# Expert tiles of an attention and expert kernel in pairs of 64-row halves, with copied words between the halves and moved weight tiles

## The chip, the core and the metric

The kernel runs on one core of a Trainium2 chip. The metric is the time of one execution on the device in microseconds (us). TensorE (PE) multiplies matrices, VectorE (DVE), ScalarE (ACT) and GpSimd (POOL) do the rest, SyncE (SP) issues most of the DMAs. Each engine works through its own instructions in order; semaphores order the engines among each other. Products go to banks of PSUM, eight in all, of 2 KB a partition.

## What is computed

An attention without softmax over 8 batches of 2496 rows, and a layer of 8 experts over all 19968 rows, each row going to the one expert with the highest logit:

```python
scores = (1.0 / S) * np.matmul(z, z.transpose(0, 2, 1))      # z: 8 x 2496 x 64
x = u * np.matmul(np.maximum(scores, 0.0) ** 2, v)           # u, v: 8 x 2496 x 256
logits = x @ w_gate + modality_bias[modality_id]             # 19968 x 8
e_idx = np.argmax(logits, axis=1)                            # gate_w: softmax at e_idx
h = np.maximum(x[mask] @ w1[e], 0.0)                         # mask: rows of expert e
out[mask] = gate_w[mask, None] * (h @ w2[e])                 # w1: 256 x 1024, w2: 1024 x 256
```

All is fp32. The kernel keeps each operand as a high part, rounded to PE's fast fp32 format, and a low part, what is left, and makes a product as three: high by high, high by low and low by high.

## The kernel before

**Attention** takes some 1340 us. A batch is cut into 5 chunks of 512 rows (the last has 448), a chunk into 10 steps. A step makes scores (`scores`, L279, three pairs), squares them, splits them into `ah` and `al` (L287 to L318), and sums products with `v` (`weigh`, L334, twelve pairs). All of these come as pairs: two matmuls, one on partitions 0 to 63 of its operands and one on 64 to 127, each to a bank of its own, so that both work at once on the two halves of PE's rows. The sums of the two banks are added when they are evacuated (L378 by ACT, L382 by DVE). A planner, which runs while the program is written, keeps a clock for ACT and DVE and gives each step a `limit` for them; what fits is issued there, the rest waits. Among that work are the logits (L434), the routing, and the split of the first experts' weights. Rows of x go to per-expert buckets `xs` in DRAM by indirect DMAs of POOL (L547).

**The experts** take the rest: 39 whole tiles of 512 rows of one expert, numbered -4 to 34, and a remainder that `run_quarter` and `run_tile` do. The tiles -4 to -1 run while the last batch's routing goes on; `between` and `put` hang pieces of it (on DVE and POOL) behind steps of these tiles. For a tile SP fetches rows (`fetch`, `xg`, L792), the 2 MB of weights of a tile two later (`fetch_weights`, L811 and L815), DVE turns the rows (`turn_blocks`, L853), and ACT and DVE split rows (`part_high` L860, `part_low` L865) and weights (L831, L835) in the course of the tile before. There are three sets of weight tiles `w1_n`, `w2_n`.

`run_tile` goes through eight slices f of 128 hidden columns. `up(t, f)` makes six products over all 128 rows of PE to one bank (L1005): two blocks of the 256 inputs by three terms, 512 columns each. ACT rectifies the sum to `hh` (L1009), DVE takes the rest to `hl` (L1010). Two slices later `down` follows for the four blocks j of 128 rows: `hh` by both parts of w2, 512 columns (L1018), and `hl` by the high part, 256 columns (L1019), into the block's bank `po`, which sums over all eight slices. So 48 + 32 products of 512 columns and 32 of 256 columns make a tile. `finish` multiplies by the gate (ACT L1033, DVE L1035), and POOL writes the rows by indirect DMAs (L1037). The engines keep the order in which the program is written there.

The first expert tile, -4, begins when the last chunk of attention ends; that chunk's rows are turned on PE by `make_last_rows` (L394, eight transposes of all 128 rows to two banks) behind the second slice.

## Time and profile before

| what | value |
| --- | --- |
| median of three runs | 2245.33 us (2245.01 to 2245.93) |
| the profiled execution's own time | 2245.74 us |
| its span in the profile | 2243.9 us |
| PE busy | 2221.6 us, 99% |
| DVE, ACT, POOL busy | 80%, 70%, 16% |
| granted clock of PE, mean | 0.997 of full speed |
| attention, without its first 20 us | 1320 us, PE busy 1319.32 |
| steady expert tiles, 1455 to 2225 us | 770 us, PE busy 770.00 |

The profile's page gives each engine's busy time, the granted clock in 40 slices, the chain of work that ended last, and the costliest groups of instructions. A timeline lists the instructions of one engine with their start, length and the idle time before them. Matmuls overlap in the pipeline of PE: a matmul of 512 columns is listed with about 390 ns, and the next one starts some 230 ns after it. What one costs is read from start to start.

### The profile page before, as it was taken

To read this page: it belongs to the slowest core of one execution; us is meant where nothing else is said; L and a number is where in the kernel's file an instruction comes from. 1 tells how busy PE (TensorE), PEld (TensorE's weight loads), DVE (VectorE), ACT (ScalarE), POOL (GpSimd) and SP (SyncE) were. 2 spreads that over 40 slices of the span, in tenths; PEclk is the share of its full clock that TensorE was granted. 3 is DMA by queue.
4 is the path that set the end of the run, shared out by engine and by line. 5 is a ranking of instruction groups with operands and counts; after the bars stand their busy time and mean duration, and the time that the engine had idled before them with its cause. 6 is when DMAs were issued, how large, how long until landed. Compare 5 with 4: busy or idle time off the path is not lost.

```text
span 2243.9 us, 44470 instructions
## 1 busy us (share of the span) xinstructions
PE 2221.6 (99%) x16874; PEld 2020.7 (90%) x16874; DVE 1804.4 (80%) x4552; ACT 1573.0 (70%) x1917; POOL 366.3 (16%) x349
## 2 busy tenths in 40 slices
PE   9999999999999999999999999999999999999996
PEld 7889999999999999999999888888888888888885
DVE  7889989989989989989989998666666666666663
ACT  7888888888888888888888873455555555555452
POOL 0000220220210210220220422211111111111111
PEclk9999999999999999999999999999999999999998
DMA  5222223222012112112111122754545454545440
GB/s 184 111 70 101 83 89 110 79 74 79 32 59 75 35 57 76 35 56 75 39 45 40 51 88 62 187 158 126 157 128 155 127 155 130 152 134 149 135 140 23
DMA packets 199602, 216.64 MB, mean 97 GB/s; under 512 B 118448, under 2 KB 166064, under 8 KB 194512
## 3 DMA queue, kind: packets, MB, share of 16 engines
q1 hardware_dynamic: 184288, 172.49, 26.3%
q0 software_dynamic: 15088, 41.21, 5.0%
q8 instruction: 134, 2.20, 0.4%
q14 instruction: 92, 0.75, 0.1%
HBM read 168.23 MB, written 62.19 MB: 103 GB/s over the span
## 4 chain that ended last, share of the span: by engine, by line
PE 59%; issue 25%; DMA 9%; POOL 3%; DVE 3%; ACT 1%; POOLq 0%; DVEq 0%; ACTq 0%
PE acc L334 44%; PE s L279 12%; DMA out_dram<-y,ids 9%; POOL out_dram L1037 3%; DVE spare L434 1%; PE ph L1005 1%; PE po L412 1%; PE po L1018 1%; DVE al L318 1%; PE po L1019 0%; DVE vl L249 0%; POOLq L1037 0%; PE warm L886 0%; DVE ah L309 0%; DVE x L382 0%
## 5 line engine op out<-in xcount | busy, mean ns | idle before, releaser
L287 ACT ACTIVATE r<-s 128x1024 f32<-128x1024 f32 (+1 forms) x395 | 397.8, 1007 | 184.5 <-PE s L279 182.7
L318 DVE TENSOR_TENSOR al<-r,ah 128x1024 fp32r<-128x1024 f32 (+1 forms) x359 | 429.8, 1197 | 84.1 <-ACT ah L309 68.9
L334 PE MATMUL acc<-ah,vh 64*128 64x512 f32 (+1 forms) x3120 | 492.8, 383 | 1.0 <-DVE ah L301 1.0
L334 PE MATMUL acc<-ah,vl 64*128 64x512 f32 (+1 forms) x3120 | 487.0, 382 | 0.0
L334 PE MATMUL acc<-al,vh 64*128 64x512 f32 (+1 forms) x3120 | 483.8, 381 | 0.0
L434 DVE SCALAR_TENSOR_TENSOR spare<-x,wgb 128x256 f32<-128x256 f32 x1280 | 462.4, 421 | 1.0
L1009 ACT ACTIVATE hh<-ph 128x512 fp32r<-128x512 f32 x312 | 186.6, 598 | 388.2 <-PE ph L1005 348.1
L1018 PE MATMUL po<-w,hh 128*128 128x512 f32 x1256 | 450.0, 394 | 0.0
L1005 PE MATMUL ph<-xh,w 128*128 128x512 f32 x1248 | 430.1, 395 | 1.4 <-DVE x L382 1.4
L293 ACT ACTIVATE r<-r 128x1024 f32<-128x1024 f32 (+1 forms) x399 | 415.6, 1042 | 3.5
L334 PEld LDWEIGHTS acc<-ah,vh 64*128 64x128 f32 x3120 | 383.3, 184 | 17.7 <-ACT x L378 1.7
L334 PEld LDWEIGHTS acc<-al,vh 64*128 64x128 f32 x3120 | 383.0, 184 | 14.6
L334 PEld LDWEIGHTS acc<-ah,vl 64*128 64x128 f32 x3120 | 381.3, 184 | 15.0 <-DVE vl L249 0.2
L1010 DVE SCALAR_TENSOR_TENSOR hl<-ph,hh 128x512 fp32r<-128x512 f32 x312 | 215.7, 691 | 219.5 <-ACT hh L1009 191.8
L279 PE MATMUL s<-zm 64*128 64x512 f32 (+1 forms) x2400 | 388.8, 386 | 0.8 <-ACT r L287 0.3
L547 POOL DMA_INDIRECT xs<-x,sloti x160 | 206.5, 1291 | 1016.2 <-DVE x L545 971.9
L1019 PE MATMUL po<-w,hl 128*128 128x256 f32 x1256 | 351.5, 280 | 0.2 <-DVE hl L1010 0.2
L279 PEld LDWEIGHTS s<-zm 64*128 64x128 f32 x2400 | 292.6, 185 | 12.3 <-ACT r L287 0.8
L309 ACT CAST ah<-r 128x1024 fp32r<-128x1024 f32 (+1 forms) x283 | 288.1, 1018 | 0.0
L1005 PEld LDWEIGHTS ph<-xh,w 128*128 128x128 f32 x1248 | 234.2, 188 | 57.6 <-DVE x L382 1.8
L1018 PEld LDWEIGHTS po<-w,hh 128*128 128x128 f32 x1256 | 235.7, 188 | 55.4
L1037 POOL DMA_INDIRECT out_dram<-y,ids x157 | 152.8, 974 | 693.7 <-DVE y L1035 659.2
(155 smaller groups left out, 1979.4 us busy)
## 6 DMA issues: line engine op xcount, KB each, us to landing
w<-w1s SPq DMA_DIRECT2D x37, 1024.0 KB
w<-w2s SPq DMA_DIRECT2D x37, 1024.0 KB
xg<-xs SPq DMA_DIRECT2D x156, 128.0 KB
vr<-in_v_dram SPq DMA_DIRECT2D x32, 512.0 KB
ut<-in_u_dram SPq DMA_DIRECT2D x32, 512.0 KB
zr<-in_zt_dram SPq DMA_DIRECT2D x40, 256.0 KB
w1s<-in_moe_w_dram SPq DMA_DIRECT2D x16, 512.0 KB
w2s<-in_moe_w_dram SPq DMA_DIRECT2D x8, 1024.0 KB
```

The lines of the kernel that those rows point to most:

```text
L279: nc.tensor.matmul(out=s[t][:, :w], lhsT=lhs, rhs=mv[halves[t], ql, :w], start=n == 0, stop=n == 2)
L287: nc.scalar.activation(out=r[:, :, :w], in_=both[:, :, :w], func=AF.Relu, scale=INV)
L293: nc.scalar.square(out=a[:, :, :w], in_=a[:, :, :w])
L309: copy(out=ah[:, :, :w], in_=st_a[g][:, :, :w])
L318: nc.vector.tensor_tensor(out=al[:, :, :w], in0=a[:, :, :w], in1=ah[:, :, :w].bitcast(F32), op=ALU.subtract)
L334: nc.tensor.matmul(out=acc[b, c][r][dh][:, :w], lhsT=V[b, k // J][y][halves[r], k % J, dh * P:(dh + 1) * P], rhs=x[halves[r], k % 2, :w], ...
L434: nc.vector.scalar_tensor_tensor(out=spare[:, k % 2, :], in0=x[:, j, 0:D], scalar=1.0, in1=wgb[:, e, :], op0=ALU.mult, op1=ALU.mult, accum ...
L1005: nc.tensor.matmul(out=ph, lhsT=lhs, rhs=rhs[:, k, :], start=n == 0, stop=n == 3 * KD - 1)
L1010: nc.vector.scalar_tensor_tensor(out=hl, in0=ph, scalar=0.0, in1=hh.bitcast(F32), op0=ALU.max, op1=ALU.subtract)
L1018: nc.tensor.matmul(out=po[j], lhsT=hh[:, s], rhs=both, start=f == 0, stop=False, skip_group_check=True)
L1019: nc.tensor.matmul(out=po[j][:, 0:D], lhsT=hl[:, s], rhs=w[:, 0, :], start=False, stop=f == KF - 1, skip_group_check=True)
L1037: nc.gpsimd.indirect_dma_start(out=out, out_offset=bass.IndirectOffsetOnAxis(ap=ids[:, j:j + 1], axis=0), in_=y, in_offset=None, bounds_ch ...
```

## The change

Every whole tile is done by a new function, `run_whole`; `run_tile` stays for the remainder.

- **Halves.** `up_half` makes two slices g and g+1 together, in pairs: one matmul on rows 0 to 63 for one slice and one on rows 64 to 127 for the other, each to its slice's bank. After six pairs (`d` = 0) each bank has half of its sum; six more pairs (`d` = 1), with the halves swapped, give the other half. `down_half` does the same with two blocks of rows and their banks `po`, for two to four slices in a go. A tile has 80 pairs of 512 columns and 32 of 256.
- **The copied word.** `change` issues on ACT a copy of one word that waits for the last matmul of a half; the first matmul of the other half on these banks waits for the copy. There are 7 in a tile, 273 in all.
- **The order.** `UPS` and `DOWNS` set it: other slices' products stand between the two halves of a bank. The last two pieces of a tile's downs run within the next tile, behind its first two halves of ups; `finish` goes with the second. In the last tile they follow at once.
- **Weights** of tile t+2 are fetched behind the second of these pieces; the split of rows and weights is hung on other steps.
- **Addresses.** The weight tiles stood at addresses that leave 32 in a division by 64 bytes, and now stand at multiples of 64 (a small tile `room` and a fourth buffer of `ids` move them). `xh`, `xl`, `hh` and `hl` stand at multiples of 64 in both.
- **Rows of the last chunk** are turned by `make_rows` in 16 transposes of 64 rows, behind the first half of ups of tile -4.
- **Start.** The strip of zeros for the warm-up is set by POOL (128 columns) and DVE (the rest); the warm-up has four pairs of 128 columns ahead of seven of 512, where it had eight of 512; the second half of z is prepared earlier.
- **Planner.** Narrower limits for DVE at the last chunk of a batch; no logits are issued in the last step of attention, they go to the first expert tiles.

```diff
-    nc.vector.memset(zeros.bitcast(F32), 0.0)
+    few = 128
+    nc.gpsimd.memset(zeros[:, 0:few].bitcast(F32), 0.0)
+    nc.vector.memset(zeros[:, few:T].bitcast(F32), 0.0)
...
+        pool.tile([P, 8], F32, name="room")
         fetch_weights(-1)
...
-        for n in range(8):
+        for n in 4 * [few] + 7 * [T]:
...
+                if f is logits and g == G - 1:
+                    continue
...
+            if c == NCH - 1 and i == NI - 3 and b < B - 1:
+                limit["D"] = after + 2.0
             if i >= NI - 2:
-                limit.update(A=after + 0.2, D=after + (0.6 if i == NI - 1 else 2.0))
+                limit.update(A=after + 0.2, D=after + (0.6 if i == NI - 1 else 1.0 if c == NCH - 1 and b < B - 1 else 2.0))
...
+    def product(out, lhs, rhs, r, key, start, stop):
+        m = ins_of(nc.tensor.matmul(out=out, lhsT=lhs, rhs=rhs, start=start, stop=stop, skip_group_check=True))
+        if key in writer and writer[key][0] != r:
+            tc.add_manual_dep(m, writer[key][1].name, data, reason="the other half's sums")
+            del writer[key]
...
+    def change():
+
+        i = ins_of(nc.scalar.copy(out=one_of[:, 0:1], in_=one_of[:, 1:2]))
+        tc.add_manual_dep(i, ended[0].name, data, reason="products of one half")
+        for key in open_keys:
+            writer[key][1] = i
+        open_keys.clear()
+
+    def up_half(t, g, d, banks):
+
+        _, xh, xl = TL[t]
+        w = weights_of(t)[0]
+        terms = [(k, q, x) for k in range(KD) for q, x in ((0, xh), (0, xl), (1, xh))]
+        for n, (k, q, x) in enumerate(terms):
+            for r, rows_of in enumerate(halves):
+                i = (r + d) % 2
+                c = slice((g + i) * P, (g + i + 1) * P)
+                product(
+                    banks[i], w[rows_of, q, k, c], x[rows_of, k, :], r, (t, "h", g + i),
+                    n == 0 and not d, n == len(terms) - 1 and d == 1,
+                )
+
+    def down_half(t, fs, h, po, d):
+
+        for p in range(0, J, 2):
+            for f in fs:
+                hh, hl = h[f]
+                w = weights_of(t)[1][:, f]
+                for x, y in ((hh, w.rearrange("p h d -> p (h d)")), (hl, w[:, 0, :])):
+                    for r, rows_of in enumerate(halves):
+                        i = p + (r + d) % 2
+                        product(
+                            po[i][:, 0:y.shape[1]], x[rows_of, i * P:(i + 1) * P], y[rows_of], r, (t, "o", i),
+                            f == 0 and not d and x is hh, f == KF - 1 and not d and x is hl,
+                        )
...
+    UPS = [(0, 0), (0, 1), (2, 0), (4, 0), (2, 1), (4, 1), (6, 0), (6, 1)]
+    DOWNS = {3: ((0, 1), 0), 4: ((0, 1), 1), 5: ((2, 3), 1), 6: ((2, 3), 0), 7: ((4, 5), 0)}
+    behind = []
+
+    def run_whole(t, ahead, extra={}):
...
+        for f, (g, d) in enumerate(UPS):
+            if not d:
+                banks[g] = [ps_h.tile([P, T], F32, tag="h", name="ph") for _ in halves]
+            up_half(t, g, d, banks[g])
+            if d:
+                h.update({g + i: rectify(x, T) for i, x in enumerate(banks.pop(g))})
+            elif f != 2:
+                change()
+            parts = {0: (0, 1), 3: (2,), 7: (3,)}.get(f, ()) if ahead and t >= -1 else ()
...
+            if behind and f < 2:
+                behind.pop(0)()
+            if f == 1 and t >= 0 and t + 2 < min(UNC + 1, MAXT):
+                fetch_weights(t + 2)
+            if f in DOWNS:
...
+                fs, d = DOWNS[f]
+                down_half(t, fs, h, po, d)
+                if f % 2:
+                    change()
...
+        def last_but_one():
+            down_half(t, (4, 5, 6, 7), h, po, 1)
+            change()
+
+        def last():
+            down_half(t, (6, 7), h, po, 0)
+            finish(t, po, f"out{t}")
+
+        behind[:] = [last_but_one, last]
+        if t == UNC - 1:
+            while behind:
+                behind.pop(0)()
...
+    last_rows = [ps_o.tile([P, J, KD, DK], F32, tag="o", name="po") for _ in halves]
+    between[0][0] += [lambda: make_rows(B - 1, NCH - 1, last_rows)]
+    between[0][1] += [lambda: [take_rows(B - 1, NCH - 1, r) for r in range(2)]]
```

PE in a steady tile, before: one slice's ups and the downs of the slice two earlier (`ph` and `po` are banks, `w_2_...` the weight tiles; a bracket names the engines whose semaphores are waited for).

```order
L1005 MATMUL ph<-xl,w_2_19206 128x512
L1005 MATMUL ph<-xh,w_2_19206 128x512 x2
L1005 MATMUL ph<-xl,w_2_19206 128x512
L1005 MATMUL ph<-xh,w_2_19206 128x512
L1018 MATMUL po<-w_2_19207,hh 128x512 [waits Activation_49]
L1019 MATMUL po<-w_2_19207,hl 128x256 [waits DVE_49]
L1018 MATMUL po<-w_2_19207,hh 128x512
L1019 MATMUL po<-w_2_19207,hl 128x256
L1018 MATMUL po<-w_2_19207,hh 128x512
L1019 MATMUL po<-w_2_19207,hl 128x256
L1018 MATMUL po<-w_2_19207,hh 128x512
L1019 MATMUL po<-w_2_19207,hl 128x256
```

After, the end of one tile and the start of the next: the first half of ups of the new tile (on the next weights), and the first of the old tile's downs that are left (`po`).

```order
L1012 MATMUL ph<-xh,w_0_18702 128x512 [waits Activation_49]
L1012 MATMUL ph<-xh,w_0_18702 128x512
L1012 MATMUL ph<-xl,w_0_18702 128x512 [waits DVE_49]
L1012 MATMUL ph<-xl,w_0_18702 128x512
L1012 MATMUL ph<-xh,w_0_18702 128x512 [waits DMAHW0_49]
L1012 MATMUL ph<-xh,w_0_18702 128x512 x3
L1012 MATMUL ph<-xl,w_0_18702 128x512 x2
L1012 MATMUL ph<-xh,w_0_18702 128x512 x2
L1012 MATMUL po<-w_2_19211,hh 128x512 [waits Activation_49]
L1012 MATMUL po<-w_2_19211,hh 128x512
L1012 MATMUL po<-w_2_19211,hl 128x256 x2
L1012 MATMUL po<-w_2_19211,hh 128x512 x2
```

Each product has become two in a row of the list ("x2"), one for each half; the six of a slice's ups have become six pairs of two slices, and the old tile's downs stand between the two halves of the new tile's ups. The waits for ACT ahead of a half's first product include the copied word.

ACT in a steady tile, before: rectified slices, with the casts of the next tile's weights (`w_0_...`) behind them.

```order
L1009 ACTIVATE hh<-ph 128x512 [waits PE_49]
L831 CAST w_0_18695<-w_0_18695 128x1024
L1009 ACTIVATE hh<-ph 128x512 [waits DVE_49,PE_49]
L831 CAST w_0_18696<-w_0_18696 128x4x256 [waits DMAHW6_49]
L1009 ACTIVATE hh<-ph 128x512 [waits DVE_49,PE_49]
L831 CAST w_0_18696<-w_0_18696 128x4x256
L1009 ACTIVATE hh<-ph 128x512 [waits DVE_49,PE_49] x2
L860 CAST xh<-xt 128x1024 [waits DVE_49]
```

After:

```order
L989 ACTIVATE hh<-ph 128x512 [waits PE_49]
L989 ACTIVATE hh<-ph 128x512
L1023 COPY c_most<-c_most 1x1 [waits PE_49,Activation_49]
L815 CAST w_1_19209<-w_1_19209 128x4x256
L1023 COPY c_most<-c_most 1x1 [waits PE_49,Activation_49]
L815 CAST w_2_19210<-w_2_19210 128x1024 [waits DMAHW5_49]
L815 CAST w_2_19210<-w_2_19210 128x1024
L1023 COPY c_most<-c_most 1x1 [waits PE_49,Activation_49]
L989 ACTIVATE hh<-ph 128x512 [waits PE_49]
L989 ACTIVATE hh<-ph 128x512
```

The rectifications come in twos, and the copied words (L1023) stand between them and the casts, each waiting for PE.

POOL at the end of the routing, before: the last scatters (`xs`) around the output DMAs of tile -2 (`out_dram`).

```order
L547 DMA xs<-x,sloti 159744x258 [waits DMASW5_49,DVE_49,Pool_49]
L1037 DMA out_dram<-y,ids 19968x256 [waits DMASW6_49,DVE_49]
L1037 DMA out_dram<-y,ids 19968x256 [waits DMASW7_49,DVE_49]
L1037 DMA out_dram<-y,ids 19968x256 [waits DMASW0_49,DVE_49]
L1037 DMA out_dram<-y,ids 19968x256 [waits DMASW1_49,DVE_49]
L547 DMA xs<-x,sloti 159744x258 [waits DMASW2_49,DVE_49]
L547 DMA xs<-x,sloti 159744x258 [waits DMASW3_49,DVE_49]
L1037 DMA out_dram<-y,ids 19968x256 [waits DMASW4_49,DMASW6_49,DMASW1_49,DMASW7_49,DMASW0_49,DVE_49]
```

After:

```order
L531 DMA xs<-x,sloti 159744x258 [waits DMASW5_49,DVE_49,Pool_49]
L531 DMA xs<-x,sloti 159744x258 [waits DMASW6_49,DVE_49]
L1081 DMA out_dram<-y,ids 19968x256 [waits DMASW7_49,DVE_49]
L1081 DMA out_dram<-y,ids 19968x256 [waits DMASW0_49,DVE_49]
L1081 DMA out_dram<-y,ids 19968x256 [waits DMASW1_49,DVE_49]
L1081 DMA out_dram<-y,ids 19968x256 [waits DMASW2_49,DVE_49]
L531 DMA xs<-x,sloti 159744x258 [waits DMASW3_49,DVE_49]
L1081 DMA out_dram<-y,ids 19968x256 [waits DMASW2_49,DMASW4_49,DMASW1_49,DMASW7_49,DMASW0_49,DVE_49]
```

One scatter fewer stands behind the four output DMAs of tile -2.

## Rows read from the trace of the kernel before

**Rows 1.** The page's first part: engine, busy us (share of the span), instructions.

```profile
PE 2221.6 (99%) x16874; PEld 2020.7 (90%) x16874; DVE 1804.4 (80%) x4552; ACT 1573.0 (70%) x1917; POOL 366.3 (16%) x349
```

**Rows 2.** Windows: length, engines' busy us (instructions), PEclk, DMA share, GB/s.

```profile
20.00:1340.00 1320.00, 1319.32 (x12292) 1263.49 (x12292) 1193.85 (x3620) 1124.47 (x1241) 196.42 (x163) 1.00 0.21 70
...
1455.00:2225.00 770.00, 770.00 (x3880) 648.24 (x3879) 503.47 (x654) 389.09 (x585) 136.21 (x140) 1.00 0.47 137
```

**Rows 3.** The page's fourth part, the chain that ended last.

```profile
PE 59%; issue 25%; DMA 9%; POOL 3%; DVE 3%; ACT 1%; POOLq 0%; DVEq 0%; ACTq 0%
```

**Rows 4.** Timeline of SP's queue, experts: start, length, instruction, count.

```profile
1699.52 1.94 SPq L792 DMA_DIRECT2D xg<-xs  x4
...
1725.29 0.36 SPq L811 DMA_DIRECT2D w<-w1s  x1
...
1744.28 1.94 SPq L792 DMA_DIRECT2D xg<-xs  x4
```

**Rows 5.** Timeline of PE, one steady tile.

```profile
1801.71 0.40 PE L1005 MATMUL ph<-xh,w 128*128 128x512 f32 x1
...
1803.11 0.40 PE L1018 MATMUL po<-w,hh 128*128 128x512 f32 x1
...
1804.52 0.40 PE L1005 MATMUL ph<-xh,w 128*128 128x512 f32 x1
```

**Rows 6.** Timeline of PE, attention, the scores that open each step.

```profile
684.80 1.02 PE L279 MATMUL s<-zm 64*128 64x512 f32 x6
...
708.60 0.79 PE L279 MATMUL s<-zm 64*128 64x512 f32 x4
```

**Rows 7.** Timeline of PE, a chunk of 448 columns.

```profile
1335.10 0.97 PE L334 MATMUL acc<-al,vh 64*128 64x448 f32 x8
...
1340.78 0.57 PE L334 MATMUL acc<-ah,vh 64*128 64x448 f32 x4
```

**Rows 8.** Timeline of PE, narrow transposes in attention.

```profile
47.03 0.65 PE L412 MATMUL po<-ident,x 64*128 64x64 f32 x16
47.49 0.47 PE L279 MATMUL s<-zm 64*128 64x512 f32 x2
```

**Rows 9.** Groups by line: count, busy us, mean ns of one, idle before, releasers.

```profile
L434 DVE SCALAR_TENSOR_TENSOR spare<-x,wgb 128x256 f32<-128x256 f32 x1280 | 462.4, 421 | 1.0
...
L1009 ACT ACTIVATE hh<-ph 128x512 fp32r<-128x512 f32 x312 | 186.6, 598 | 388.2 <-PE ph L1005 348.1 <-issue 35.1 <-DVE p_last L670 4.9
...
L831 ACT CAST w<-w 128x1024 fp32r<-128x1024 f32 x148 | 154.0, 1042 | 0.0
...
L473 ACT ACTIVATE ex<-sh 128x160 f32<-128x160 f32 (+2 forms) x9 | 2.9, 321 | 9.9 <-DVE sh L467 9.8
```

**Rows 10.** Windows, experts, after a fetch of weights.

```profile
1734.00:1736.00 2.00, 2.00 (x12) 1.64 (x11) 1.75 (x2) 0.91 (x1) 0.00 (x0) 1.00 0.10 39
```

**Rows 11.** Timeline of PE, start; brackets: idle before, its releaser.

```profile
1.47 3.78 PE L886 MATMUL warm<-zeros 64*128 64x512 f32 x16 [1.47 <-DVE zeros L96]
...
11.61 0.50 PE L279 MATMUL s<-zm 64*128 64x512 f32 x2 [0.24 <-ACT zm L229]
12.34 0.73 PE L279 MATMUL s<-zm 64*128 64x512 f32 x4 [0.22 <-DVE zm L234]
```

**Rows 12.** Attention's products (L334), the waits before them: us, times.

```profile
  ACT x L378: 1.7, 7
```

**Rows 13.** Windows, the first expert tiles.

```profile
1340.00:1455.00 115.00, 113.39 (x583) 95.11 (x580) 92.50 (x258) 44.45 (x72) 30.94 (x31) 1.00 0.45 118
```

**Rows 14.** Timeline of POOL, the last scatters.

```profile
1418.08 0.97 POOL L547 DMA_INDIRECT xs<-x,sloti  x1 [0.30 <-issue]
1419.36 1.60 POOL L547 DMA_INDIRECT xs<-x,sloti  x1 [0.31 <-issue]
```

**Rows 15.** Timeline of PE, the last pairs of attention, the halves apart.

```profile
1341.99 0.36 PE L334 MATMUL acc<-ah,vh 64*128 64x448 f32 x1
1342.00 0.36 PE L334 MATMUL acc<-al,vh 64*128 64x448 f32 x1
```

More of the change, by code (lines that the diff above doesn't have):

```diff
@@ L568, in tile_attention_moe @@
     skip = t8("skip")
+    one_of = small.tile([1, 4], F32, name="c_most")
     def choose():
@@ L573, in choose @@
         nc.vector.tensor_tensor(out=cnt, in0=base[one], in1=base0[one], op=ALU.subtract)
-        one_of = small.tile([1, 4], F32, name="c_most")
         most, who, at = one_of[:, 0:1], one_of[:, 1:2], one_of[:, 2:4]
@@ L883, in tile_attention_moe @@
         warm = [bank_tile([P, T], "warm") for _ in halves]
-        for n in range(8):
+        for n in 4 * [few] + 7 * [T]:
             for x, h in zip(warm, halves):
-                nc.tensor.matmul(out=x, lhsT=zeros[h, 0:P], rhs=zeros[h, :], start=True, stop=True)
+                nc.tensor.matmul(out=x[:, 0:n], lhsT=zeros[h, 0:P], rhs=zeros[h, 0:n], start=True, stop=True)
         prep_z_high(0, 0)
@@ L952, in tile_attention_moe @@
             for n in new_h:
-                by[n] = "A" if n > 2 and clock["A"] + 2.1 * scale <= limit["A"] or clock["D"] > limit["D"] else "D"
+                free = n > 2 and (i, c) != (NI - 1, NCH - 1) and clock["A"] + 2.1 * scale <= limit["A"]
+                by[n] = "A" if free or clock["D"] > limit["D"] else "D"
                 clock[by[n]] = max(clock[by[n]], now) + (1.05 if by[n] == "A" else 0.7) * scale
@@ L994, in tile_attention_moe, with rectify @@
         weight_tiles(wp, n)
+    def rectify(ph, nt):
+        hh = mp.tile([P, T], F32R, tag="hh", bufs=4, name="hh")[:, 0:nt]
+        hl = mp.tile([P, T], F32R, tag="hl", bufs=4, name="hl")[:, 0:nt]
+        nc.scalar.activation(out=hh, in_=ph, func=AF.Relu)
+        nc.vector.scalar_tensor_tensor(out=hl, in0=ph, scalar=0.0, in1=hh.bitcast(F32), op0=ALU.max, op1=ALU.subtract)
+        return hh, hl
     def up(t, f):
@@ L1006, in up @@
                 n += 1
-        hh = mp.tile([P, T], F32R, tag="hh", bufs=4, name="hh")[:, 0:nt]
-        hl = mp.tile([P, T], F32R, tag="hl", bufs=4, name="hl")[:, 0:nt]
-        nc.scalar.activation(out=hh, in_=ph, func=AF.Relu)
-        nc.vector.scalar_tensor_tensor(out=hl, in0=ph, scalar=0.0, in1=hh.bitcast(F32), op0=ALU.max, op1=ALU.subtract)
-        return hh, hl
+        return rectify(ph, nt)
+    ended, writer, open_keys = [], {}, []
+    def product(out, lhs, rhs, r, key, start, stop):
[3 more added lines that the diff above has]
+            del writer[key]
+        if key not in writer:
+            writer[key] = [r, None]
+        open_keys.append(key)
+        ended[:] = [m]
@@ L1085, in run_quarter, with run_tile @@
         finish(t, po, f"out{t}{part}")
-    def turn_at(t):
-        return 4 if t == 1 - EARLY else KF - 2
-    def run_tile(t, ahead, extra={}, part=""):
+    def run_tile(t, part=""):
         if len(TL[t]) < 3:
@@ L1115, in run_tile @@
         finish(t, po, f"out{t}{part}")
+    assert KF == 8 and J == 4
+    UPS = [(0, 0), (0, 1), (2, 0), (4, 0), (2, 1), (4, 1), (6, 0), (6, 1)]
+    DOWNS = {3: ((0, 1), 0), 4: ((0, 1), 1), 5: ((2, 3), 1), 6: ((2, 3), 0), 7: ((4, 5), 0)}
+    behind = []
+    def run_whole(t, ahead, extra={}):
+        if len(TL[t]) < 3:
+            turn(t)
+        po, h, banks = [], {}, {}
+        for f, (g, d) in enumerate(UPS):
[7 more added lines that the diff above has]
+            parts = {0: (0, 1), 3: (2,), 7: (3,)}.get(f, ()) if ahead and t >= -1 else ()
+            if f < KF - 1:
+                for q in parts:
+                    part_weights_high(t + 1, q)
+                    part_weights_low(t + 1, q)
+            if ahead and f == 6:
+                part_high(t + 1)
+                part_low(t + 1)
+            if behind and f < 2:
[3 more added lines that the diff above has]
+            if f in DOWNS:
+                if not po:
+                    po += [ps_o.tile([P, 2 * D], F32, tag="o", name="po") for _ in range(J)]
+                fs, d = DOWNS[f]
+                down_half(t, fs, h, po, d)
+                if f % 2:
+                    change()
+            if f == KF - 1:
+                for q in parts:
+                    part_weights_high(t + 1, q)
+                    part_weights_low(t + 1, q)
+            for e in extra.get(f, ()):
+                e()
+            if ahead and f == 5:
+                turn_blocks(t + 1)
+        def last_but_one():
[8 more added lines that the diff above has]
+                behind.pop(0)()
@@ L1148, in tile_attention_moe @@
             assert next(planning, planning) is planning
[L1149 to L1150 removed]
         if t == UNC - 1 and MAXT > UNC:
             fetch(UNC, 0, 1)
[L1153 removed]
+        run_whole(t, t + 1 < min(UNC + 1, MAXT), between.get(t + EARLY, {}))
     if MAXT > UNC:
```

50 lines of the change are left out of this document (9 added, 41 removed).

## The prediction, made before the changed kernel ran

> **What bounds the kernel now.** The first view is the page's table of busy time: TensorE (PE) is busy 99% of the span [rows 1]. The second cuts the span into stages: attention from 20 to 1340 us, then the experts to 2225 us, with PE busy 1319.32 of 1320.00 and 770.00 of 770.00 at a granted clock of 1.00, the upper of the two levels; ACT has 389.09 of 770 in the expert stage [rows 2]. The chain of waits, the third, says the same: 59% PE, 25% "issue", DVE and ACT 3% and 1% [rows 3]. So in both stages time leaves only where PE's own instructions get fewer or cheaper, and any wait that PE gains is paid in full. The rest of the reading is of the distance between starts on PE, by operand form, since a matmul's own length overlaps the next one's.
>
> **The steady expert tile, before.** SP issues a tile's row fetch at 1699.52 and, two tiles on, at 1744.28: 22.38 us a tile [rows 4]. In it six full-height 512-column products of one slice go from 1801.71 to 1803.11, 0.2333 each, and four down steps of 512 and 256 columns from 1803.11 to 1804.52, 0.3525 each, so 0.2333 and 0.1192 [rows 5]. 48 and 32 of the wide, 32 of the narrow make 18.67 + 3.81 = 22.48, which is the period to 0.1: nothing but products is in it.
>
> **What a pair of halves costs.** The attention stage is made of such pairs already. Seven steps of 15 pairs of 512 columns run from 684.80 to 708.60: 0.2267 a pair [rows 6]. With 448 columns 28 pairs run from 1335.10 to 1340.78: 0.2029 [rows 7]. With 64 columns eight pairs run from 47.03 to 47.49: 0.058 [rows 8]. The 512-column pair therefore does the work of a full-height 512-column product in 0.0066 us less.
> For the 256-column pair there is no row. Below it is half a wide pair, 0.113. Above it is the straight line from 64 to 512 columns: 0.058 + 192/448 x 0.169 = 0.130. Between: 512 columns at 2.4 GHz take 0.2133, so the wide pair has 0.0133 beside its columns, and with these kept the narrow pair takes 0.1067 + 0.0133 = 0.120. I take that, since it lies nearest to the full-height 256-column product of 0.1192.
>
> **The change, step by step.**
> 1. A tile becomes 80 wide and 32 narrow pairs: 80 x 0.2267 + 32 x 0.120 = 21.97 us, 0.41 less than 22.38. Over 39 tiles: -15.9 us. With 0.113 it is -24.6, with 0.130 it is -3.4.
> 2. The copied words. Each of seven changes of halves in a tile makes PE wait for a one-word copy on ACT that itself waits for PE. Its price is about that of ACT's smaller rows: 0.32 for 160 columns is the nearest [rows 9], and it can't be above that. It lies on the path only where PE has nothing between the last product of one half and the first of the other on the same banks. The order puts a block between: a half of ups is 6 pairs, 1.36 us; a half of downs on two slices 8 pairs, 1.39; the four-slice half of the old tile 2.78. ACT takes its work in order, and ahead of a copy stand casts of weights at 1.04 each or two rectifications of 0.60 [rows 9]. The casts are issued a block earlier, so they run while PE makes the block that the copy waits for: two under 2.78, one under 1.39, one under 1.36. Followed by hand through one tile, the smallest slack is 0.6 (rectified slices before the downs that use them). ACT grows from 389/770 of 22.38 = 11.3 us a tile to at most 11.3 + 7 x 0.32 = 13.5 of 22. I take 0; if the cover were gone, 273 x 0.3 = 82 us would be the whole of it.
> 3. The weights of tile t+2 are fetched 6.9 us into tile t, where SP did it at the tile's start. In before they are issued at 1725.29, and the DMA rate is down to 39 GB/s by 1734 to 1736 [rows 4, 10]: 10.7 us. Issued at 6.9 they are there by 17.6 of 22, and the first cast of them is in the next tile. The row fetches of the next tile stand ahead of them on SP as before. 0.
> 4. The weight tiles' addresses move from 32 to 0 modulo 64 bytes. In before the wide product costs 0.2333 where the weights are the stationary operand (ups) and 0.3525 - 0.1192 where they are the moving one (downs), so no row shows that the address costs anything: 0 beyond step 1, and a rival below.
> 5. The start. PE waits 1.47 us for the strip of zeros that the warm-up reads, and 0.24 and 0.22 for the second half of z [rows 11]. A strip cut to a quarter on two engines gives back half of the first, the earlier preparation the others: 0.7 + 0.5 = 1.2 us, -0.5 to -2.
> 6. The planner's limits at a batch's last chunk: seven stalls of 1.7 us in all behind the evacuation [rows 12]: -1.0, between 0 and -2.
> 7. The first four tiles, where DVE still does routing. Before, PE is busy 113.39 of the 115 us there, so it loses 1.6 [rows 13]. After, the last chunk's rows are turned by 16 narrow transposes already behind the first half of ups: PE is there some 1.25 us before the evacuation has ended. DVE has about eight more logits ahead of tile -3's turned rows, each 462.4/1280 = 0.36 of it [rows 9], 2.9 us with some 0.5 covered by the products still to run: 2.4 late. Slices are rectified in twos, so the second hl is later: 1.1 in small waits. On POOL the last scatter stands behind the output DMAs of tile -2, whose end now lies behind two halves of the next tile's ups, 2 x 1.36 = 2.7 later; one scatter less, 1.28 at POOL's spacing [rows 14], stands between. So it goes out 1.4 later, tile 0's row fetch waits for it, and I count 1.2 of that on the path. 1.25 + 2.4 + 1.1 + 1.2 - 1.6 = +4.3, 0 to +7.
> 8. The end. The last tile has nothing to put between, so two changes stand open: each the end of the last product, the copy and the way back, 0.16 + 0.32 + 0.07 = 0.55: +1.1.
> Sum: -15.9 - 1.2 - 1.0 + 4.3 + 1.1 = -12.7. The profiled execution took 2245.74 (a span of 2243.9 and 1.84 around it, which the change leaves), so 2233.0; it lay 0.41 above the median of 2245.33, so 2232.6 for a median.
>
> **A rule against it.** In the rows, the second half of a pair starts 0.01 us after the first [rows 15], and the pair's cadence is 0.2267 all the same. The Trainium skill, "TensorE: Matmul & The Clock Gate", section "Measured speedup vs the span model", has it that a pack of tiles spans one matmul's duration and about 4 ns for each further tile. By that rule a pair costs a full product and 4 ns, an estimate of 112 x 4 ns = 0.45 us more a tile, +17.5 in all; the trace agrees only if the cheap cadence of attention comes from something else than the halves, which is the second rival.
>
> **The rivals.**
> A. The forecast, some 13 us faster.
> B. The narrow pairs eat the gain: at 0.130 each the tile gives 0.09, and the sum is -3.4 - 2.2 + 5.4 = -0.2: 2245. For it: the 64-column pairs take 0.058, of which columns are 0.027, so short pairs carry more than 0.0133 [rows 8]. Against: full-height narrow products show no such load (0.1192 against 0.2333), and it would take the line's very end.
> C. Slower: a pair on the experts' operands is no cheaper than the full product. Attention has other operands, at other addresses, and no full-height product of its own, so no row holds both forms on the same data. Then a pair costs 0.2333 or 0.1192 and the second half's start, 0.01: 112 x 0.01 = 1.1 us a tile, +44 us and the 3 of steps 5 to 8, 2292; with a mere 3.6 ns (0.41/112) above the assumed pairs' price the gain is gone, and from there it is slower. Against it: 0.2267 over 105 pairs with weights loaded anew for each, as in the experts.
> D. Slower: the copied words are late. One wait of 0.41 us exposed a tile takes the gain away, and ACT's queue could do that where a cast of 1.04 stands ahead of a copy with 1.36 of cover: one exposed 0.7 a tile gives 39 x (0.7 - 0.41) = +11 and the 3 of steps 5 to 8, 2259. Against it: ACT is half idle, and only three of seven copies have a cast ahead.
> That the change doesn't do what it says: the order listing shows halves, banks and waits as described, so no chance of its own.
>
> **Chances and range.** A 0.68, B 0.14, C 0.08, D 0.10. The likeliest is A: 2232.6 us. Its own range, with step 1 at -24.6 and steps 5 to 8 at their best, goes to 2218; at its worst (0.126 a narrow pair, first tiles +7) to about 2244. B lies at 2241 to 2250, C and D beyond. 2218 to 2250 leaves out C, D and little else: 0.18. About 0.2%, 4.5 us, is what a measurement of this kernel can tell from no change: faster (below 2240.8) 0.70, same 0.13, slower 0.17.
>
> **What the profile after would show.** The fetch issues of SP 21.9 to 22.0 apart instead of 22.38; six pairs of ups in 1.36 and a narrow pair's cadence of 0.12 in the downs. In PE's waits no name of the copied word (ACT, c_most) with more than a few us in all, and those at the last tile. Two or three stalls of 1 to 3 us between 1342 and 1440 behind DVE. Attention's cadence unchanged at 0.2267. The prediction is wrong if the period is above 22.3 with PE waiting for nothing (B, C), or if PE waits for the copies in each tile (D).

## The result and the profile after

The changed kernel takes 2253.89 us, the median of 7 runs (2250.22 to 2256.08), against 2245.33 for the kernel before; the ratio is 1.0037, with a 95% interval of 1.0027 to 1.0048. It is 8.6 us slower where 12.7 us faster was forecast, and it lies outside the range. Its profiled execution took 2251.67, 5.93 more than before's 2245.74. The page's first part and the chain that ended last, of the changed kernel:

```profile
PE 2218.0 (99%) x21256; PEld 1906.7 (85%) x21256; DVE 1780.8 (79%) x4552; ACT 1603.8 (71%) x2190; POOL 364.6 (16%) x350
...
PE 94%; DVE 3%; ACT 1%; issue 1%; DMA 0%; POOL 0%; SPq 0%; DVEq 0%; POOLq 0%; ACTq 0%
```

PE bounds it as before [rows 1, 3], and it is busy 3.6 us less in a span 6.0 longer. So there are waits that before didn't have. Where they lie, the timeline of PE tells: the first product of the experts, and the first of the last, quarter tile.

```profile
1339.53 0.37 PE L336 MATMUL acc<-ah,vl 64*128 64x448 f32 x2
1339.73 0.39 PE L1012 MATMUL ph<-xh,w 64*128 64x512 f32 x1
...
2223.99 0.33 PE L1116 MATMUL ph<-xh,w 128*128 128x128 f32 x1
```

In before's trace the same two products:

```profile
1342.69 0.50 PE L1005 MATMUL ph<-xh,w 128*128 128x512 f32 x1
...
2218.52 0.22 PE L1072 MATMUL ph<-xh,w 128*128 128x128 f32 x1
```

The period of a steady tile is read from SP's queue, which issues a tile's row fetch once a tile; timeline of SP of the changed kernel:

```profile
1637.48 1.93 SPq L776 DMA_DIRECT2D xg<-xs  x4
...
1640.88 0.54 SPq L795 DMA_DIRECT2D w<-w1s  x1
1648.13 0.57 SPq L799 DMA_DIRECT2D w<-w2s  x1
1659.69 1.94 SPq L776 DMA_DIRECT2D xg<-xs  x4
```

From 1637.48 to 1659.69, and over all tiles on the mean, it is 22.21 us where before had 22.38 [rows 4]. Between the two products of PE lie 39 whole tiles. What that stretch is longer than 39 periods is what the first tiles lose:

| us | before | after | forecast of the difference | difference |
|---|---|---|---|---|
| start and attention, to the first expert product | 1342.69 | 1339.73 | -2.2 (steps 5, 6) | -3.0 |
| 39 periods | 872.8 | 866.1 | -15.9 (step 1) | -6.7 |
| rest of the stretch: first tiles, open changes at the end | 3.0 | 18.2 | +5.4 (steps 7, 8) | +15.2 |
| quarter tile and last stores | 25.3 | 25.9 | 0 | +0.5 |
| profiled execution | 2245.74 | 2251.67 | -12.7 | +5.9 |

The last row is the execution's own time, which is 1.9 and 1.8 us more than the span that the rows above add up to.

The median lies another 2.2 above the profiled execution; the last experiment bears on that. Two steps failed, then: the tile gave less than half, and the first tiles cost nearly three times what was counted.

What PE waited for in the expert stage (us in total, times, longest), of the changed kernel:

```profile
PE ph L1012 <- ACT xh L845: 2.7, 2, 2.1
PE ph L1012 <- DVE x L384: 2.5, 1, 2.5
PE po L1012 <- DVE hl L990: 2.2, 1, 2.2
PE ph L1012 <- ACT c_most L1023: 1.8, 1, 1.8
PE ph L1012 <- DVE xl L850: 1.5, 2, 0.8
PE po L1012 <- ACT c_most L1023: 0.7, 2, 0.3
```

Before's list of the same stretch has 1.4 us for x and 0.2 for hl. All but the last line lie between 1339 and 1440, 10.7 us; the last line is the copied word (c_most) in the last tile, at 2218.98 and 2222.39. In the tiles between, PE waits for nothing: the copied words stay hidden there.

The longest wait is the stage's second product. Timeline of PE, after, and below it the wait for x of before:

```profile
1342.63 0.49 PE L1012 MATMUL ph<-xh,w 64*128 64x512 f32 x1 [2.50 <-DVE x L384]
```

```profile
1345.74 0.50 PE L1005 MATMUL ph<-xh,w 128*128 128x512 f32 x1 [1.38 <-DVE x L382]
```

A pair writes two banks at once, and the second of them is one that DVE was still evacuating (x): after one product, at 1339.73, PE stood still. In before six full-height products went to the first bank and covered a part of the same wait.

The next three have this behind them. At 1377.42 PE waits 1.83 us for a copied word. Timeline of ACT (in brackets the idle time before and what ended it):

```profile
1372.54 0.87 ACT L1077 ACTIVATE part<-po,gate 128x256 f32<-128x256 f32 x2 [0.66 <-DVE y L1079]
1377.00 0.28 ACT L457 ACTIVATE ex<-sh 128x96 f32<-128x96 f32 x1 [3.60 <-DVE sh L451]
1377.19 0.40 ACT L1023 COPY c_most<-c_most 1x1 f32<-1x1 f32 x2
```

ACT isn't busy there; it stands still for 3.60 us at the routing's exponential, which waits for DVE, and two copied words are queued behind it. At 1406.99 PE waits 2.20 us for hl, on whose engine, DVE, the routing's plan is ahead (timelines of PE and DVE):

```profile
1406.99 0.39 PE L1012 MATMUL po<-w,hl 64*128 64x256 f32 x2 [2.20 <-DVE hl L990]
...
1405.85 0.49 DVE L658 TENSOR_REDUCE p_off<-p_ge 1x42 f32<-1x336 f32 x1
1406.27 1.27 DVE L990 SCALAR_TENSOR_TENSOR hl<-ph,hh 128x512 fp32r<-128x512 f32 x2
```

At 1438.55 it waits 2.13 us for tile 0's xh, whose rows were fetched at 1430.19 instead of 1422.65, behind a last scatter that POOL issued at 1427.58 instead of 1419.36 [rows 14]. And then it runs slowly (windows; the number before the DMA share is the granted clock):

```profile
1410.00:1415.00 5.00, 5.00 (x56) 4.23 (x54) 3.54 (x6) 2.53 (x5) 1.95 (x2) 1.00 0.90 277
1435.00:1440.00 5.00, 2.11 (x22) 1.34 (x20) 2.72 (x3) 2.55 (x5) 0.00 (x0) 1.00 0.99 186
1440.00:1445.00 5.00, 5.00 (x38) 4.17 (x38) 3.78 (x5) 2.68 (x4) 0.00 (x0) 0.66 1.07 367
```

After a stretch in which PE is busy 2.11 us of 5, the granted clock is 0.66 in the next: it stood at its lower level, half, for two thirds of that time, 5 x 0.34 = 1.7 us lost. Waits and clock make 12.4 of the 18.2, with the 0.7 at the end 13.1. Of the rest some 2 us belong to the same nine waits: a wait is listed only from the end of the product before it, 0.16 us after the next would have started (0.39 against 0.23), and the first product behind it takes some 0.1 us more to the next. What is left wasn't followed up.

### The profile page after: what moved, and what is told of

It reads as the page before. It is cut to its first block, busy times and chain, and to the rows that moved or that the text cites. A ratio compares the mean times of both kernels' runs of the same rounds, so it can differ in the third digit from the quotient of the medians.

```text
span 2249.9 us, 53772 instructions
## 1 busy us (share of the span) xinstructions
PE 2218.0 (99%) x21256; PEld 1906.7 (85%) x21256; DVE 1780.8 (79%) x4552; ACT 1603.8 (71%) x2190; POOL 364.6 (16%) x350
## 3 DMA queue, kind: packets, MB, share of 16 engines
q8 instruction: 168, 2.75, 0.5%
## 4 chain that ended last, share of the span: by engine, by line
PE 94%; DVE 3%; ACT 1%; issue 1%; DMA 0%; POOL 0%; SPq 0%; DVEq 0%; POOLq 0%; ACTq 0%
PE acc L336 45%; PE po L1012 18%; PE ph L1012 18%; PE s L281 12%; DVE spare L418 1%; PE po L396 1%; DVE al L320 0%; DVE hl L990 0%; DMA xg<-xs 0%; PE warm L871 0%; DVE xl L850 0%; DVE xt L838 0%; DVE w L819 0%; POOL out_dram L1081 0%; ACT r L285 0%
## 5 line engine op out<-in xcount | busy, mean ns | idle before, releaser
L1012 PE MATMUL po<-w,hh 64*128 64x512 f32 x2496 | 453.3, 391 | 0.7 <-ACT c_most L1023 0.7
L1012 PE MATMUL ph<-xh,w 64*128 64x512 f32 x2496 | 446.6, 389 | 7.2 <-ACT xh L845 2.7
L336 PE MATMUL acc<-ah,vl 64*128 64x512 f32 (+1 forms) x3120 | 424.9, 382 | 0.0
L1012 PE MATMUL po<-w,hl 64*128 64x256 f32 x2496 | 366.2, 276 | 2.2 <-DVE hl L990 2.2
L336 PEld LDWEIGHTS acc<-ah,vh 64*128 64x128 f32 x3120 | 299.6, 184 | 58.3 <-DVE ah L303 1.3
L336 PEld LDWEIGHTS acc<-al,vh 64*128 64x128 f32 x3120 | 299.8, 184 | 52.5
L336 PEld LDWEIGHTS acc<-ah,vl 64*128 64x128 f32 x3120 | 292.6, 184 | 54.5 <-DVE vl L251 0.2
L1012 PEld LDWEIGHTS ph<-xh,w 64*128 64x128 f32 x2496 | 251.8, 184 | 48.2 <-ACT xh L845 3.4
L1012 PEld LDWEIGHTS po<-w,hh 64*128 64x128 f32 x2496 | 252.3, 185 | 39.8 <-ACT c_most L1023 1.3
L1012 PEld LDWEIGHTS po<-w,hl 64*128 64x128 f32 x2496 | 251.8, 185 | 11.1 <-DVE hl L990 3.1
```

The lines of the kernel that those rows point to most:

```text
L336: nc.tensor.matmul(out=acc[b, c][r][dh][:, :w], lhsT=V[b, k // J][y][halves[r], k % J, dh * P:(dh + 1) * P], rhs=x[halves[r], k % 2, :w], ...
L1012: m = ins_of(nc.tensor.matmul(out=out, lhsT=lhs, rhs=rhs, start=start, stop=stop, skip_group_check=True))
```

## The experiments

**Is it the halves or the addresses?** Two kernels undo one of them each. The first is the kernel before, with nothing but the addresses moved to multiples of 64 bytes.

```
+        pool.tile([P, 8], F32, name="room")
         fetch_weights(-1)
...
-        ids = mp.tile([P, J], I32, tag="ids", bufs=3, ...
+        ids = mp.tile([P, J], I32, tag="ids", bufs=4, ...
```

> The kernel before with the addresses of the change alone: weights, fetched rows and output rows at multiples of 64 bytes, products over full height. Theory A, the address costs time in full-height products too: the period falls below 22.38 by over 0.05 us, total under 2243. Theory B: 22.38 and 2245.3 within 1 us.

It took 2240.24, a ratio of 0.9979 (0.9970 to 0.9989). Timeline of SP:

```profile
1541.70 1.93 SPq L792 DMA_DIRECT2D xg<-xs  x4
...
1563.94 1.94 SPq L792 DMA_DIRECT2D xg<-xs  x4
```

A period of 22.24 with full-height products in the order of before. The two lines move the fetched rows and the output rows too; that the weights make the difference is argued from PE, which reads none of the other two and waits for nothing in a steady tile. The second is the changed kernel, order and addresses kept, with full-height products in place of the halves:

```
-            for r, rows_of in enumerate(halves): ...  product(banks[i], w[rows_of, q, k, c], x[rows_of, k, :], ...)
+            nc.tensor.matmul(out=banks[d], lhsT=w[:, q, k, c], rhs=x[:, k, :], ...)
-        i = ins_of(nc.scalar.copy(out=one_of[:, 0:1], in_=one_of[:, 1:2]))     # the copied word
```

> The changed kernel with its order, addresses, start and planner, but each block made of full-height products of one slice in place of two halves, and without the copied words. Theory A (a pair of halves costs the same as the full-height product at the same addresses; the gain of 0.17 a tile was the addresses'): period 22.2 to 22.25 as in the changed kernel, the stalls of the first tiles stay (DVE and the order make them), so about 2252 (2254 less 0.8 at the end). Rival (halves are cheaper): period 22.35 or more, 2258 and above.

It took 2242.79, 0.9989 (0.9979 to 0.9998) of before and 11.1 us less than the changed kernel. The stalls of the first tiles, which were expected to stay, went in large part with the halves; the stretch of 39 tiles starts and ends here (timeline of PE):

```profile
1339.51 0.50 PE L1020 MATMUL ph<-xh,w 128*128 128x512 f32 x1
...
2214.52 0.23 PE L1087 MATMUL ph<-xh,w 128*128 128x128 f32 x1
```

Its tile against that of the changed kernel, the same block of six products and the block of downs behind it; timeline of PE, first with full height (a row of the downs is one product), then in halves (a row is a pair):

```profile
1607.96 0.39 PE L1020 MATMUL ph<-xh,w 128*128 128x512 f32 x1
...
1609.33 0.40 PE L1033 MATMUL po<-w,hh 128*128 128x512 f32 x1
...
1610.73 0.39 PE L1020 MATMUL ph<-xh,w 128*128 128x512 f32 x1
```

```profile
1641.10 0.40 PE L1012 MATMUL ph<-xh,w 64*128 64x512 f32 x2
...
1642.47 0.41 PE L1012 MATMUL po<-w,hh 64*128 64x512 f32 x2
...
1645.26 0.41 PE L1012 MATMUL ph<-xh,w 64*128 64x512 f32 x2
```

Six full-height products take 1.37 us and six pairs take 1.37. Four down steps take 1.40, eight in pairs 2.79. Both kernels have a period of 22.21. So a pair of halves costs what the full-height product costs on the same operands, and the 0.17 us of the tile are the addresses' (0.14) and the order's (0.03).

The reverse was tried too, the changed kernel with its weights back at 32 modulo 64:

> The changed kernel with all weights at 32 modulo 64, as before. Theory A (address costs the same whether a product has 128 rows or is two halves): period 22.21 + 0.14 = 22.35, time 2254 + 5 = 2259. Rival B (halves suffer more from the address, as two reads of a row run at once): period 22.6 or more, 2268 and above. Rival C (address does nothing to halves): 22.21, 2254.

2273.08, a ratio of 1.0126 (1.0111 to 1.0142), with a period of 22.65: far more than the address. The next question bears on that.

**Can the first tiles be mended?** The changed kernel, with tiles -4 to -1 made by before's code and only the 35 others in halves:

```
-        run_whole(t, ...)
+        (run_early if t < 0 else run_whole)(t, ...)      # run_early: run_tile of before
```

> The first four expert tiles (-4 to -1) are done as before the change: full-height products, the order, the eight full transposes, finish at the tile's end. Tiles 0 to 34 run in pairs of halves. Theory 1, the loss lies in the first four tiles (four stalls behind DVE and ACT, the late rows of tile 0, and the clock's fall after it): about 2245.3 - 3.0 (attention ends 3.0 us earlier) - 35 x 0.17 (the tile's period 22.21 against 22.38) + 0.8 (two open changes at the end) = 2237, and a spread of under 1.5 us between executions, since no idle time of over 2 us is left for the clock to fall after. Rival, the loss comes with the whole order (pieces behind, later fetches, copied words) wherever it runs: 2248 to 2254.

2253.74, no better than the changed kernel. The long waits were gone but for one of 1.1 (hl), and the steady period had become 22.57, with hl late in nearly every tile. A second kernel, the changed one without the room tile, which puts one of the three sets of weights at 32 modulo 64, had the same trouble:

> The changed kernel without the small tile that moves one of the three sets of weights: the set 0 (tiles -4 to -1 and every third tile from 2 on) stands at 32 modulo 64 bytes again, the sets 1 and 2 at multiples of 64. Theory A, the address costs time in pairs: the periods of the tiles on set 0 are longer than those of their neighbours, 22.21, by 0.1 us or more, the total by over 1.2 us. Theory B, it costs nothing: all periods 22.21 to 0.02, total unchanged at 2250 to 2256.

2271.37 (1.0119, 1.0102 to 1.0136), with a period of 22.5 to 22.7 in all but two tiles and hl late in tiles of all three sets. Its time tells nothing of the address then, nor does the reverse above. Where the 0.36 of a tile goes is seen on ACT. The same three steps of a tile, first of e1, then of the changed kernel (timeline of ACT):

```profile
1575.71 1.05 ACT L833 CAST w<-w 128x1024 fp32r<-128x1024 f32 x1
1577.68 0.19 ACT L1041 COPY c_most<-c_most 1x1 f32<-1x1 f32 x1 [0.93 <-PE po L1030]
1579.83 1.09 ACT L1007 ACTIVATE hh<-ph 128x512 fp32r<-128x512 f32 x2 [1.96 <-PE po L1030]
```

```profile
1651.13 1.04 ACT L815 CAST w<-w 128x1024 fp32r<-128x1024 f32 x1
1652.49 0.19 ACT L1023 COPY c_most<-c_most 1x1 f32<-1x1 f32 x1 [0.32 <-PE po L1012]
1653.83 1.09 ACT L989 ACTIVATE hh<-ph 128x512 fp32r<-128x512 f32 x2 [1.14 <-PE ph L1012]
```

From the cast's start to the copied word it is 1.97 instead of 1.36 us, to the rectification 4.12 instead of 2.70, and ACT is idle before both, waiting for PE. Yet PE's products follow each other at the usual distance all the while; it is their semaphores that reach ACT late, by 0.6 and 1.4 us. The trace's own times of PE's semaphore say the same: it is raised 0.63 us behind the end of the product that ends at 1576.97 and 1.45 behind that of the next, at 1578.36, and 0.01 behind the same two in the changed kernel. So ACT wasn't late itself. hl comes later by that, and PE waits for it a block on.

Two causes were tried that had something on their side. In the changed kernel's steady tiles the second half of a pair starts 17 ns after the first, in e1 3 ns. An added product of 64 columns on the lower rows set them apart:

> The kernel of e1 (early tiles as before, whole tiles in halves), in which hl is late in nearly every tile (period 22.57 instead of 22.21), with one added product of 64 columns on the lower rows at the start of tiles 0, 10, 20 and 30, so that the lower half of each later pair runs tens of ns behind the upper one. Theory P: the late semaphores of e1 come of the two halves ending together (3 ns apart in e1, 17 ns in the changed kernel, where hl isn't late): then the period falls to 22.21 and the time to about 2253.7 - 36 x 0.36 = 2241. Rival Q: the distance between halves has nothing to do with it: period 22.57, time 2254.

2254.44 (1.0039, 1.0024 to 1.0055). The halves now lay 30 to 50 ns apart for two tiles behind the first added product, and ACT's waits there were those of e1 (1.96 us at 1489.28, with 50 ns): rival Q. The distance isn't the cause.

The other is traffic. The late semaphores fall where SP has just issued the second half of the next weights (w2s, 1572.71 in e1) and POOL sends off the tile's four outputs (1574.10 to 1577.93). Two kernels part them, the first (e9) makes the w2 fetch wait for a later product, the second (e10) the first of the outputs for the same product. The edit of e9:

```
+                if f == 5 and ...:
+                    fetch_weights(t + 2, (1,), ended[0])     # w2 alone, behind the first downs on slices 2 and 3
```

> The kernel of e1, in which PE's semaphores reach ACT up to 1.4 us late once a tile, while the second half of the next weights (w2) and the four output transfers are under way together. Here the w2 fetch waits until the block of the tile's first downs on slices 2 and 3 is done, some 5 us later. Theory W (the weights' burst delays the semaphores): they are on time where the outputs go alone, period 22.21, time 2253.7 - 13 = 2241; or they are late where the burst now lies, with its own wait. Theory O (the outputs do it): period 22.57, time 2254.

> The kernel of e1 with the four output transfers of a tile held back until the first downs on slices 2 and 3 are done, some 5 us later; the w2 fetch stays where it was. Theory O: semaphores on time beside the weights, period 22.21, time 2241, or late at the outputs' new place. Theory W: late as before, 22.57, 2254. If both together are needed, this one and e9 both come to 22.21.

2240.82 (0.9981, 0.9971 to 0.9990) and 2240.79 (0.9979, 0.9970 to 0.9988): each alone takes the 13 us back, and both have a period of 22.21. Timeline of ACT in e9, the same steps:

```profile
1553.29 0.19 ACT L1047 COPY c_most<-c_most 1x1 f32<-1x1 f32 x1 [0.32 <-PE po L1036]
1554.62 1.09 ACT L1013 ACTIVATE hh<-ph 128x512 fp32r<-128x512 f32 x2 [1.14 <-PE ph L1036]
```

The waits are those of the changed kernel to 0.01. So in e1 it takes the weights' transfer and the outputs together. That isn't enough by itself, and the mechanism stays open: why the profiled execution of the changed kernel, which has the same two together in each tile, and the full-height kernel e7 show no late semaphore, these runs don't settle.

**The address with halves, again.** With semaphores on time the question could be asked properly: e9 with all weights at 32 modulo 64.

> The kernel of e9 (halves, early tiles as before, w2 later, semaphores on time) with all weights at 32 modulo 64 bytes, as before. If the address costs the same whether a product has 128 rows or is two halves, the period goes from 22.21 to 22.35 and the time from 2240.8 to about 2246. If halves suffer more from it, or the late semaphores come back, 22.5 and above, 2252 and more. If halves don't feel it, 2241.

2247.78 (1.0012, 1.0002 to 1.0021), 7.0 above e9. Timeline of SP, e12:

```profile
1539.21 2.79 SPq L794 DMA_DIRECT2D xg<-xs  x4
...
1561.68 4.45 SPq L794 DMA_DIRECT2D xg<-xs  x4
...
1584.04 2.56 SPq L794 DMA_DIRECT2D xg<-xs  x4
```

That is 22.41 a tile (44.83/2), and PE waits for nothing in a steady tile. The four cases together, us a tile:

| | weights at 32 modulo 64 | at 0 modulo 64 |
|---|---|---|
| full height, order of before | 22.38 | 22.24 (e3) |
| full height, new order | not tried | 22.21 (e7) |
| halves, new order | 22.41 (e12) | 22.21 (after, e9, e10) |

The address is worth 0.20 a tile with halves in the new order and 0.14 with full height in the old one; as the fourth case wasn't run, whether the halves or the order make the difference is open. At 0 modulo 64, where both forms stand in one order, halves are worth nothing.

**Start and planner.** The kernel before with the changed start and planner alone:

> The kernel before with the start and the planner's limits of the change, experts as before. My reading of the two traces: attention's last product ends 3.0 us earlier than before (1339.7 against 1342.7). If all of it arrives: 2242.3. If the logits that are put off into the first expert tiles give part of it back there: 2243 to 2245. Above 2245.3 if they cost more than the start and the limits bring.

2243.08 (0.9992, 0.9983 to 1.0002). Its first expert product starts at 1339.94 instead of 1342.69, 2.75 earlier, and waits of 0.9 (hl) and 0.5 (xl) in the second tile give part of it back. With the addresses too:

> The kernel before with the weights at multiples of 64 bytes and the change's start and planner limits, without halves and without the new order of the tiles. Addresses alone gave 5.1 us (2240.24) and the start and planner 2.3 (2243.08). If the two act in different stages and add, 2245.0 - 5.1 - 2.3 = 2237.6 with a tile's period of 22.24. If they share a cause, it stays near 2240.

2238.20 (0.9956 to 0.9980 of before, ratio 0.9968): the two add. And without the rule that holds logits back:

> The kernel of e5 (2238.2) without the rule that holds logits back from the last step of attention, which in e4 and e5 ends attention 2.9 us earlier but is followed by waits of 1.1 (hl) and 0.65 us (xl) behind DVE in the second early tile. If those come of the logits that were held back, they shrink and the attention's end stays about where it is: 2237. If the rule is what frees DVE at attention's end, its end goes back by about 1 us: 2238 to 2239.

2237.69 (0.9965, 0.9953 to 0.9977), the same within the intervals: the two waits shrink to 0.3, and PE waits 1.4 instead of 0.3 for the evacuated x. Both kernels beat the changed kernel and the one before, and neither has a half or a copied word in its expert tiles.

**The spread, and what is left of the first tiles.** The changed kernel with nothing but e9's edit:

> The changed kernel with the one edit of e9: w2 is fetched some 5 us later. In the profiled execution of the changed kernel the semaphores are on time and the period is 22.21, but its runs spread over 6 us and their median lies 2.2 above the profiled one. If late semaphores in some tiles of some runs make that, this one comes to 2250 to 2252 with a spread of 1 us, and what it has above e9 (2240.8) is the first tiles' alone, about 10. If it stays at 2254 with its spread, the spread is of something else.

2254.68 (2253.46 to 2256.53; 1.0042, 1.0027 to 1.0056): no gain, period 22.21, so late semaphores are not what the changed kernel loses in. Against e9 (2240.82), which differs from it only in tiles -4 to -1, it is 13.9 us slower: that is what those four tiles cost in halves and the new order. Its waits are those of the changed kernel to 0.2 us (10.9 against 10.7), but its profiled execution is 3.7 us longer (2255.40). The windows say where:

```profile
1375.00:1380.00 5.00, 3.17 (x24) 2.34 (x22) 3.35 (x15) 1.09 (x5) 1.95 (x2) 0.81 0.24 84
1380.00:1385.00 5.00, 5.00 (x46) 4.16 (x44) 2.41 (x4) 1.83 (x5) 0.00 (x0) 0.85 0.00 0
1405.00:1410.00 5.00, 2.79 (x22) 1.84 (x20) 4.72 (x17) 1.09 (x2) 2.67 (x4) 0.88 0.22 79
1410.00:1415.00 5.00, 5.00 (x42) 4.21 (x42) 3.08 (x5) 1.33 (x3) 1.22 (x2) 0.78 0.71 206
1440.00:1445.00 5.00, 2.61 (x12) 1.93 (x14) 3.89 (x5) 3.04 (x5) 0.00 (x0) 0.79 0.89 260
1445.00:1450.00 5.00, 5.00 (x48) 4.22 (x48) 2.53 (x3) 2.29 (x4) 0.00 (x0) 0.86 1.23 279
```

Here the clock falls after three waits, each time for 1.7 us of loss ((0.19 + 0.15) x 5 the first time), where in the changed kernel's profiled execution only the third was followed by that: its windows from 1375 to 1385 and from 1405 to 1415 have a clock of 1.00. Up to tile 0 the two programs do the same work with the same waits. So whether a stop of about 2 us is followed by the lower clock differs from one execution to the next, at 1.7 us each; the longest, of 2.50 at 1342, wasn't in either. The profiled execution of the changed kernel, with one fall, took 2251.67; none would give 2250.0 and all three 2255.1, and its runs go from 2250.22 to 2256.08 with the median between two and three. The mean granted clock of each run bears it out: 0.997 of full speed in the run of 2250.22, 0.996 in that of 2251.67, 0.995 in the four from 2252.40 to 2254.93, 0.994 in that of 2256.08, where one fall is worth 1.7/2250 = 0.0008. In e3, e7, e9 and e10 every run has 0.997, and the runs spread over less than 2 us. How many falls each run had can't be counted in three digits. The Trainium skill, "TensorE: Matmul & The Clock Gate", section "Part 1: The HAM clock gate", has it that the number of slow products at a start differs between runs of one kernel. It says so of the start alone, which no run here tests; what these two traces show is of waits in mid-kernel.

## Why the prediction was wrong

- **Step 1 is the step that failed.** "The 512-column pair therefore does the work of a full-height 512-column product in 0.0066 us less" compared attention's pairs [rows 6] with the experts' products [rows 5]: other operands at other addresses. On the same operands the two cost the same, 1.37 for six of either (e7, after). The narrow pair, the term held to be uncertain, came out at 0.117 and did no harm. The tile gained 0.17 instead of 0.41, 6.7 us instead of 15.9, and none of it by halves. Why a pair in attention takes 0.2267 and one in the experts' ups 0.228 to 0.232 (six in 1.37 or 1.39) stays open.
- **Rival C was right in its condition and wrong in its price.** It named the gap ("no row holds both forms on the same data") and had 0.08. The pair does cost the full product, without the 0.01 that C put on top of it. The rule of the Trainium skill ("TensorE: Matmul & The Clock Gate", "Measured speedup vs the span model") has a pack span one product and some 4 ns for each further tile. The traces agree with the first half; of the second, an estimate of 0.45 us a tile, they show nothing: between e7 and the changed kernel there is less than 0.01.
- **Step 4 failed.** That "no row shows that the address costs anything" was true of the rows and no reason for 0: before had all its weights at 32 modulo 64, ups and downs alike, so no row could show it. The addresses are worth some 5 us (e3: 5.1 below the median of before, 4.7 below before's runs made beside it), 0.14 of the 0.17 that the tile gained. That they also explain the tile that the pairs were to explain is why steps 1 and 4 had to be told apart by a run.
- **Step 7 was too small, +4.3 for about +14.5.** Full-height products in the same order lose 8.9 in that stretch, by the same reckoning as in the table (875.0 - 866.1), against 3.0 before: the order, with the logits put off, costs 5.9, near what the step counted. Halves and copied words cost 9.3 more (18.2 - 8.9, with 0.7 of it at the end), and of that the step had only 1.1 for later hl. For the evacuation of x it counted 1.25, but PE waits 2.50 (1.16 in e7), since a pair needs both banks. Missing were the copied word behind an exponential that waits for DVE (1.83), hl behind the plan (2.20; 1.66 in e7) and the lower clock after a wait (1.7); tile 0's fetch was 7.5 us later, not 1.4, and its wait 2.9 instead of 1.2.
- **Step 2 held in 35 tiles, by the argument given; it failed in the first four.** The cover was counted in ACT's busy time, with casts of 1.04 ahead of a copy. What made the copy late was an instruction of 0.28 that itself waited 3.60: a queue is late by what its instructions wait for, too.
- **Step 3 held in the changed kernel, by luck.** The step had both parts of the weights issued 6.9 us into the tile. In the tile that starts at 1641.10, w1 goes 0.2 us before its first product and w2, which waits for the last products of the tile before, 7.0 us into it, and there it meets the outputs, which the step didn't look at. In e1 that meeting cost 13 us.
- **Rivals B and D.** B's condition didn't come about (0.117 a narrow pair). D's did, but not in each tile: once in the first tiles. In e1 and e2 something is late in nearly each tile, but it is hl, behind late semaphores.
- **Steps 5, 6 and 8 held**: -3.0 for -2.2 in 5 and 6 together, and 0.7 for 1.1 in the two open changes.

## What to carry to other kernels

A price read in one stage need not hold in another whose operands differ; where a forecast rests on such a transfer, the run that settles it is the cheap one that changes the form and nothing else. When a change bundles a form with an address, undo each alone: here the two lines that move addresses made nearly the whole gain of the tile. And a wait that is added to an engine's queue is hidden only if nothing ahead of it in that queue waits longer than the cover, which busy time doesn't show.

## What was not expected of the hardware

- Weight tiles that start at 0 instead of 32 modulo 64 bytes (with the fetched and output rows moved along) took 0.14 us off a tile of 22.38 with full-height products and 0.20 off one of 22.41 with halves.
- In e1, PE's semaphores reached ACT 0.6 and 1.4 us late while a 1 MB fetch of weights and four indirect output transfers were under way together, with PE's products at their usual distance. Either one moved by some 5 us put them right, worth 13 us; in the changed kernel the same two transfers together left them on time.
- Waits of PE of 1.8 to 2.3 us were followed by a stretch at the lower clock in some executions and not in others, 1.7 us lost each time.
